# Chunked attention and a SwiGLU layer on one core: turning the second tile's tokens on VectorE and through DRAM instead of on TensorE

## The chip, the core and the metric

The kernel runs on 1 of the 8 cores of one Trainium2 chip. A core has TensorE (PE in the profile, its weight loads PEld), VectorE (DVE), ScalarE (ACT), GpSimd (POOL) and SyncE (SP), whose queue here issues nearly every DMA. The metric is the device time of one execution in microseconds (us), as the median of the runs shown.

## The reference

Attention runs within chunks of 64 tokens, for 8 batches, 8 heads and 576 tokens of head size 64. Its result, as 4608 tokens of 512 channels, goes through a normalised SwiGLU layer with 1536 hidden features, all in float32:

```python
scores = scale * np.matmul(q_c, k_c.transpose(0, 1, 2, 4, 3))
attn = np.exp(scores - np.max(scores, axis=-1, keepdims=True))
attn = attn / (np.sum(attn, axis=-1, keepdims=True) + 1e-09)
x = np.matmul(attn, v_c)            # then (B, H, S, D) -> (B * S, H * D)
...
rms = np.sqrt(np.mean(x * x, axis=-1, keepdims=True) + 1e-06)
xn = x / rms * rms_g
g = xn @ w_gate
silu = g * (1.0 / (1.0 + np.exp(-g)))
val = xn @ w_val
out = silu * val @ w_out
```

## The kernel before, in words

The 4608 tokens are 9 tiles of 512. Tiles 0, 1 and 2 are computed with plain products; the last six go in three pairs, by a scheme with seven products in place of eight, whose weight sums are prepared during tiles 1 and 2. Every float32 product is made of three products of a high and a low part (`xh`, `xl` for tokens, `parts` for weights).

A plain tile has 12 steps `f`. In each, TensorE makes the gate product `ps_g` (12 matmuls), the value product `ps_v` (12) and, one step late, the down product into the four banks `acc` (12, `down(f - 1)`). ScalarE applies the SiLU (`sg`), VectorE multiplies (`sg`), and the two split the result into `gh` and `gl`. The gate and value banks come from a pool of two, so `ps_g` of step f + 1 can start only when the SiLU of step f has read its bank. At the end of a tile, `evacuate` copies the four `acc` banks to `o`, on VectorE and ScalarE in turn, and SP stores them (`out_dram<-o`).

Tokens come in units of 256, two to a tile. Attention for the next tile runs in between the steps of the present one: scores (`ps_s<-kt,qt`), softmax, the values (`ps_o`), the normalisation, and then the tokens have to be turned, so that channels lie on partitions, before they are split into `xh` and `xl`. There are three ways to turn:

- Tile 0, units 0 and 1: TensorE transposes (`x_turn_unit`).
- Tile 1, units 2 and 3, made during tile 0: `norm_unit` writes them into the tile `x`; at the end of tile 0, `x_transpose` turns them with 16 TensorE transposes of 128x128, eight before `down(10)` and eight before `down(11)`, and ScalarE and VectorE split from PSUM.
- Units 4 and on: VectorE transposes 32x32 blocks in place in a tile `xu` (`turn_x`), one DMA stores it to DRAM (`away_x`), and four DMAs read it back into `x` with the blocks in their places (`turn_x_back`). The splits then read SBUF.

Also in tile 0, the float64 weights are converted, piece by piece (`conv_step`), on ScalarE and VectorE. From the converted parts, `save_plain` and `sides` in tile 1 store what the pairs need to DRAM (`wsd`, `osd`; `wsd<-parts` of 512 KB and `osd<-parts` of 256 KB each for the plain parts).

The order of the work is set by a scheduler, apart from stretches in `manual_schedule`, which keep the written order on the engines named. From tile 1 on, TensorE is in such a stretch. SP's queue is filled by the scheduler throughout tiles 0 to 2: it may place a DMA well ahead of, or behind, its place in the code. What stands in a queue is issued strictly in that order, and an entry that waits holds back all behind it.

In tile 2 the scores of unit 6 stand right behind the gate and value products of the first step; its tokens' loads are `qt`, `kt`, `vt` in `load_unit(6)`, which stand in the code at the start of tile 2.

Of the kernel before, what the change touches and what calls it, by code (L numbers as in the profile page):

```python
# [13 lines left out]
AF = mybir.ActivationFunctionType  # L14
# [71 lines left out]
def tile_chunk_attn_swiglu(  # L86
# [47 lines left out]
    def bank(pool, name):  # L134
        return pool.tile([P, 512], F32, tag=pool_tag[id(pool)], name=name)
# [320 lines left out]
    def turn_x(u):  # L456
        src = state["xu", u].rearrange("p q a s d -> p (q a s) d")
        nc.vector.transpose(src, src)
        src = state["xu", u].rearrange("p q a s d -> p q (a s d)")
        away = state["away", u] = dram.tile([P, 2 * DM], F32, name=f"away_x{u}")  # L460
        nc.sync.dma_start(away, src.rearrange("p q c -> p (q c)"))

    def turn_x_back(u, x):
        away = state["away", u]
        back = away.rearrange("(t p) (q r) -> q p t r", t=4, q=4)
        half = blocks(x)[:, 4 * (u % 2) : 4 * (u % 2) + 4]
        for q in range(4):
            nc.sync.dma_start(
                half[q * Q : (q + 1) * Q].rearrange("p t a c -> p t (a c)"), back[q]
            )  # L470

    def blocks(x):

        return x.rearrange("p s c -> p (s c)").rearrange("p (n a c) -> p n a c", a=NDT, c=2 * Q)
# [19 lines left out]
        nc.scalar.activation(spent, xs, AF.Square, accum_out=ss)  # L494
        return root(ss, "ri")

    def norm_unit(u, banks):
        rs = state.pop(("rs", u))
        subs = [state.pop(2 * u + s) for s in range(2)]
        first = 2 * u % NSUB  # L500
        xu = x[:, first : first + 2]
        xv = xu.rearrange("p s (j b a d) -> p j s b a d", j=2, b=2, d=Q)
        for j in range(2):
            for b in range(2):
                nc.vector.tensor_tensor(
                    xv[:, j, :, b],
                    banks[j].rearrange("p s (a b d) -> p b s a d", b=2, d=Q)[:, b],
                    rs[:, :, :, j].broadcast_to([P, 2, NPAIR, Q]),
                    op=ALU.mult,
                )  # L510
        ss = small.tile([P, 2], F32, name="ss_u")
        for s, st in enumerate(subs):
            spent = st["e"].rearrange("p a j k -> p (a j k)")
            nc.scalar.activation(spent, xu[:, s], AF.Square, accum_out=ss[:, s : s + 1])
        ri = root(ss, "ri_u")
        for s in range(2):
            nc.gpsimd.tensor_scalar(xu[:, s], xu[:, s], ri[:, s : s + 1], None, op0=ALU.mult)

    def x_split(dt, pt, cols):
        g = g_col[:, dt : dt + 1]  # L520
        hi, lo = xh[dt][:, cols], xl[dt][:, cols]
        if len(pt.shape) == 3:
            hi, lo = (w.rearrange("p (n c) -> p n c", c=2 * Q) for w in (hi, lo))
        nc.scalar.mul(hi, pt, g)
        nc.vector.scalar_tensor_tensor(
            lo, pt, g, hi.bitcast(F32), op0=ALU.mult, op1=ALU.subtract
        )

    def x_transpose(dts):
        for dt in dts:  # L530
            pt = bank(ps_a, "ps_x")
            for s in range(NSUB):
                nc.tensor.transpose(
                    pt[:, s * P : (s + 1) * P], x[:, s, dt * P : (dt + 1) * P], ident
                )
            x_split(dt, pt, slice(0, TT))

    def x_turn_unit(u, d, pool):
        pt = state["xt", u, d] = bank(pool, "ps_x")
# [96 lines left out]
    def gate_and_value(f):  # L636
        return up(wgh, wgl, f, "ps_g"), up(wvh, wvl, f, "ps_v")

    def gated(f, at, then, ps=None):
        pg, pv = ps or gate_and_value(f)  # L640
        if 0 in at:
            then()
        sg = tmp_tile("sg")
        gh = gp.tile([P, TT], F32R, name="gh")
        gl = gp.tile([P, TT], F32R, name="gl")
        with urgent():
            nc.scalar.activation(sg, pg, AF.Silu)
        if 1 in at:
            then()
        with urgent():  # L650
            nc.vector.tensor_tensor(sg, pv, sg, op=ALU.mult)
            nc.scalar.copy(gh, sg)
        if 2 in at:
            then()
        with urgent():
            nc.vector.tensor_tensor(gl, sg, gh.bitcast(F32), op=ALU.subtract)
        return gh, gl
# [561 lines left out]
        conv_sign(3)  # L1219
    conv_at[0] = EARLY  # L1220

    for t in range(PLAIN):
        if t == 1:
            ordered = tc.manual_schedule(engines={mybir.EngineType.PE})
            ordered.__enter__()
            at = {}
            for n, u in enumerate((4, 5)):
                for k, f in enumerate(unit_steps(u, x)):
                    at.setdefault(2 + 9 * n + FIRST_STEPS[k], []).append(f)
            half = Steps(at)  # L1230
            st = last.open("st", 1)
            made = [[] for _ in range(NF + 2)]
            for i in range(NPR):
                steps = sides(i, st)
                made[max(2 * i - 1, 0)].append(steps[0])
                made[2 * i].append(steps[1])
                made[2 * i + 1].append(steps[2])
        elif t == 2:
            st = last.open("st2", 1)
            x2 = st.tile([P, NSUB, DM], F32, tag="x2", bufs=1, name="x2")  # L1240
            at = {}
            for n, u in enumerate(range(2 * PLAIN, 2 * PLAIN + 4)):
                for k, f in enumerate(unit_steps(u, (x, x2)[n // 2])):
                    after_it = {1: LATE_STEPS, 2: LONG_STEPS}.get(n, UNIT_STEPS)
                    at.setdefault(max(UNIT_AT[n] + after_it[k], 0), []).append(f)
            for i in range(OUT_FIRST):
                for k, todo in enumerate(out_sides(i, st)):
                    at.setdefault(4 * i + 2 + k, []).extend(todo)
            one, two, late = x_sides(x, x2, st)
            for n, f in enumerate(one):  # L1250
                at.setdefault(15 + n, []).append(f)
            at.setdefault(22, []).extend([two[0], two[4]])
            at.setdefault(23, []).extend(two[1:4])
            early = {n: list(todo) for n, todo in enumerate(late)}
            for n, i in enumerate(range(OUT_FIRST, NPR)):
                for k, todo in enumerate(out_sides(i, st)):
                    early.setdefault(6 + 5 * n + k, []).extend(todo)
            at.setdefault(14, []).append(lambda: ring_load_ahead(0))
            half = Steps(at)
        acc = [ps_acc.tile([P, DM], F32, tag="acc", name=f"acc{s}") for s in range(NSUB)]  # L1260
        prev = None
        for f in range(NF):
            if f in gs:
                conv_step()
                g = gs.pop(f)
            else:
                g = gated(f, CONVS[f % 2], conv_step, ps.pop(f, None))
            if t == 0:
                if f in (0, 5):
                    u = 2 + (f == 5)  # L1270
                    load_unit(u)
                    sc = two_banks(ps_a, "ps_s")
                    for i in (2 * u, 2 * u + 1):
                        scores(i, sc)
                    if f:
                        softmax_rows(u, sc)
                    else:
                        softmax_whole(u, sc)
                elif f in (2, 7):
                    for i in (2 * u, 2 * u + 1):  # L1280
                        att_transpose(i)
                elif f in (3, 8):
                    o = two_banks(ps_a, "ps_o")
                    for i in (2 * u, 2 * u + 1):
                        att_values(i, o)
                    norm_unit(u, o)
                if f == NF - 1:
                    x_transpose((0, 1))
            elif t == 1 and f == NF - 1:
                for dt in range(NDT):  # L1290
                    x_split(dt, blocks(x)[:, :, dt], slice(0, TT))
            if t == 1:
                if f % 2 == 0:
                    save_plain(f // 2)
                for todo in made.pop(0):
                    todo()
            if t:
                half()
            if prev is not None:
                down(acc, f - 1, *prev)  # L1300
            if t:
                half()
            prev = g
        if t == 0:
            x_transpose((2, 3))
        down(acc, NF - 1, *prev)
        for s in range(NSUB):
            evacuate(acc, t, s)
# [84 lines left out]
```

## Time and profile before

| | |
|---|---|
| median of 3 runs | 899.57 us (899.17 to 899.58) |
| the profiled execution's own time | 898.29 us |
| its span in the trace | 896.5 us |
| TensorE busy | 880.0 us (98%) |
| VectorE busy | 607.6 us (68%) |
| ScalarE busy | 454.1 us (51%) |
| GpSimd busy | 185.7 us (21%) |

The span is what the trace covers from the first instruction to the last; the execution's own time has 1.8 us more around it. Busy shares are means over the span. A matmul's end in the trace is modelled, so matmuls that follow each other overlap a little, and it is the distance between two starts that tells what one costs.

### The profile page before, as it was taken

To read this page: it belongs to the slowest core of one execution; us is meant where nothing else is said; L and a number is where in the kernel's file an instruction comes from. 1 tells how busy PE (TensorE), PEld (TensorE's weight loads), DVE (VectorE), ACT (ScalarE), POOL (GpSimd) and SP (SyncE) were. 2 spreads that over 40 slices of the span, in tenths; PEclk is the share of its full clock that TensorE was granted. 3 is DMA by queue.
4 is the path that set the end of the run, shared out by engine and by line. 5 is a ranking of instruction groups with operands and counts; after the bars stand their busy time and mean duration, and the time that the engine had idled before them with its cause. 6 is when DMAs were issued, how large, how long until landed. Compare 5 with 4: busy or idle time off the path is not lost.

```text
span 896.5 us, 17443 instructions
## 1 busy us (share of the span) xinstructions
PE 880.0 (98%) x6828; PEld 720.6 (80%) x6828; DVE 607.6 (68%) x965; ACT 454.1 (51%) x772; POOL 185.7 (21%) x157
## 2 busy tenths in 40 slices
PE   5999999999999999999999999999999999999998
PEld 4778888888888888888887888888878888888886
DVE  6999955364568745985677997556769953334776
ACT  5988934253446464454456645435547522222452
POOL 0004050342200000233233003333330014323200
PEclk8899999999999999999999999999999999999999
DMA  9889999777978855698977877677667794445442
GB/s 349 328 318 336 332 337 347 239 255 235 303 252 234 267 170 196 250 298 294 320 240 265 318 301 286 245 277 249 232 231 286 281 355 171 152 154 199 179 165 95
DMA packets 85794, 231.84 MB, mean 259 GB/s; under 512 B 8912, under 2 KB 45264, under 8 KB 71504
## 3 DMA queue, kind: packets, MB, share of 16 engines
q1 hardware_dynamic: 84656, 230.20, 73.1%
q8 instruction: 54, 0.88, 0.4%
q10 hardware_dynamic: 1056, 0.52, 0.2%
q14 instruction: 28, 0.23, 0.1%
HBM read 167.25 MB, written 63.44 MB: 257 GB/s over the span
## 4 chain that ended last, share of the span: by engine, by line
PE 94%; DVE 2%; ACT 2%; DMA 0%; issue 0%; POOL 0%; ACTq 0%; DVEq 0%
PE ps_b L857 11%; PE ps_a L857 11%; PE ps_c L857 11%; PE acc L664 11%; PE ps_g L627 11%; PE ps_v L627 10%; PE ps_b L1070 6%; PE ps_c L1070 6%; PE ps_d L857 5%; PE ps_a L1070 5%; PE ps_d L1070 3%; PE ps_o L426 2%; PE ps_s L299 2%; PE ps_o L484 1%; DMA x<-qT_dram 0%; ACT raw L196 0%
## 5 line engine op out<-in xcount | busy, mean ns | idle before, releaser
L857 PE MATMUL ps_b<-xp,wr 128*128 128x512 f32 x432 | 104.7, 391 | 0.1
L857 PE MATMUL ps_c<-xp,wr 128*128 128x512 f32 x432 | 104.0, 390 | 0.0
L857 PE MATMUL ps_a<-xp,wr 128*128 128x512 f32 x432 | 103.8, 390 | 0.0
L627 PE MATMUL ps_g<-xh,parts 128*128 128x512 f32 x288 | 97.2, 399 | 0.1
L857 PEld LDWEIGHTS ps_b<-xp,wr 128*128 128x128 f32 x432 | 80.5, 188 | 17.4 <-issue 0.5
L857 PEld LDWEIGHTS ps_c<-xp,wr 128*128 128x128 f32 x432 | 80.9, 188 | 16.9
L627 PE MATMUL ps_v<-xh,parts 128*128 128x512 f32 x288 | 94.5, 389 | 0.0
L857 PEld LDWEIGHTS ps_a<-xp,wr 128*128 128x128 f32 x432 | 80.8, 188 | 17.0
L664 PE MATMUL acc<-parts,gh 128*128 128x512 f32 x288 | 90.2, 394 | 0.0
L945 POOL TENSOR_TENSOR g<-u,u 128x512 f32<-128x512 f32 x18 | 23.2, 1289 | 251.9 <-DVE u L941 141.3
L627 PEld LDWEIGHTS ps_g<-xh,parts 128*128 128x128 f32 x288 | 54.7, 190 | 12.7 <-ACT parts L237 0.6
L627 PEld LDWEIGHTS ps_v<-xh,parts 128*128 128x128 f32 x288 | 54.1, 188 | 11.2
L977 ACT CAST gh<-g 128x512 fp32r<-128x512 f32 x72 | 43.6, 622 | 37.8 <-PE ps_c L1070 13.5
L664 PEld LDWEIGHTS acc<-parts,gh 128*128 128x128 f32 x288 | 53.1, 188 | 11.3
L982 DVE TENSOR_TENSOR gl<-g,gh 128x512 fp32r<-128x512 f32 x72 | 49.3, 692 | 16.2 <-PE ps_a L1070 5.7
L913 ACT ACTIVATE p<-p 128x512 f32<-128x512 f32 x36 | 22.7, 632 | 70.0 <-POOL p L935 60.4
L935 POOL TENSOR_TENSOR p<-p,p 128x512 f32<-128x512 f32 x36 | 46.9, 1313 | 53.9 <-DVE rs L387 35.6
L627 PE MATMUL ps_g<-xl,parts 128*128 128x512 f32 x144 | 56.8, 395 | 0.1
L664 PE MATMUL acc<-parts,gl 128*128 128x512 f32 x144 | 56.1, 390 | 0.0
L627 PE MATMUL ps_v<-xl,parts 128*128 128x512 f32 x144 | 56.0, 389 | 0.0
L922 DVE TENSOR_TENSOR u<-ps_b,p 128x512 f32<-128x512 f32 x36 | 24.6, 687 | 41.5 <-PE ps_b L857 38.0
L857 PE MATMUL ps_d<-xp,wr 128*128 128x512 f32 x216 | 52.3, 391 | 0.0
(151 smaller groups left out, 1706.7 us busy)
## 6 DMA issues: line engine op xcount, KB each, us to landing
wr<-wsd SPq DMA_DIRECT2D x63, 1024.0 KB, 7.0
wo<-osd SPq DMA_DIRECT2D x30, 1024.0 KB, 7.6
raw<-w_up_dram SPq DMA_DIRECT2D x12, 1024.0 KB, 9.5
vt<-v_dram SPq DMA_DIRECT2D x18, 512.0 KB, 7.2
wsd<-parts SPq DMA_DIRECT2D x18, 512.0 KB, 8.3
qt<-qT_dram SPq DMA_DIRECT2D x17, 512.0 KB, 5.6
kt<-kT_dram SPq DMA_DIRECT2D x17, 512.0 KB, 6.6
away_e<-e SPq DMA_DIRECT2D x28, 256.0 KB, 3.5
```

The lines of the kernel that those rows point to most:

```text
L299: nc.tensor.matmul(st["s"][j][c * CH : (c + 1) * CH, pr], st["q"][rows, pr, tok : tok + CH], st["k"][rows, pr, tok : tok + CH], start=True ...
L426: nc.tensor.matmul(st["o"][(2 * c + t) * Q : (2 * c + t + 1) * Q, h * D : (h + 1) * D], eT[c][rows, t, h], vt[rows, c, h], start=True, sto ...
L627: nc.tensor.matmul(ps, a[f][:, cols], b[dt], start=(dt == 0 and i == 0), stop=(dt == NDT - 1 and i == 2),)
L664: nc.tensor.matmul(acc[s], a[:, cols], b, start=(f == 0 and i == 0), stop=(f == NF - 1 and i == 2),)
L857: nc.tensor.matmul(ps, w[:, a, m, cols], xp[:, b, kt], start=start and kt == 0 and i == 0, stop=stop and kt == 1 and i == 2, skip_group_ch ...
L913: nc.scalar.activation(t, t if src is None else src, AF.Silu)
L922: nc.vector.tensor_tensor(kp["u2"], b["b"], kp["p1"], op=add)
L935: nc.gpsimd.tensor_tensor(kp["p5"], kp["p1"], kp["p5"], op=add)
L945: nc.gpsimd.tensor_tensor(g[:, 0, 1], kp["u2"], kept[0]["u2"], op=mult)
L977: nc.scalar.copy(gh, src)
L982: nc.vector.tensor_tensor(gl, src, pair[0].bitcast(F32), op=ALU.subtract)
L1070: nc.tensor.matmul(banks[m][name], w[:, (0, 1, 0)[k], m * P : (m + 1) * P], (gh, gh, gl)[k], start=opens and i == 0 and k == 0, stop=not ( ...
```

## The change

Units 2 and 3 are now turned as the later units are, but in place: `norm_unit` writes the unit into the half of `x` in the block order that the later units use, VectorE transposes it there, SP stores that half to DRAM and reads it back into the same half in four reads. Unit 2 is turned at step 7 of tile 0 and read back at step 8; unit 3 is turned and read back at step 10. `x_transpose` is gone. The scaling of unit 3 by its norm goes from GpSimd to ScalarE (`shared`); that of unit 2 stays on GpSimd. At the last step of tile 0 the gate and the splits of the next tile keep their written order on ScalarE and VectorE. The rest of the diff puts output rows in order on the host.

```diff
-    def norm_unit(u, banks):
+    def norm_unit(u, banks, shared):
...
-        first = 2 * u % NSUB
-        xu = x[:, first : first + 2]
-        xv = xu.rearrange("p s (j b a d) -> p j s b a d", j=2, b=2, d=Q)
+        xu = x[:, 2 * u % NSUB : 2 * u % NSUB + 2].rearrange("p s c -> p (s c)")
+        xu = state["xu", u] = xu.rearrange("p (q a s d) -> p q a s d", q=4, a=NDT, s=2)
+        xv = xu.rearrange("p q (j b) s d -> p j s b q d", b=2)
+        xs = xu.rearrange("p q a s d -> p s (q a) d")
...
-            spent = st["e"].rearrange("p a j k -> p (a j k)")
-            nc.scalar.activation(spent, xu[:, s], AF.Square, accum_out=ss[:, s : s + 1])
+            spent = st["e"].rearrange("p a j k -> p (a j) k").rearrange("p a (b d) -> p (a b) d", d=Q)
+            nc.scalar.activation(spent, xs[:, s], AF.Square, accum_out=ss[:, s : s + 1])
         ri = root(ss, "ri_u")
         for s in range(2):
-            nc.gpsimd.tensor_scalar(xu[:, s], xu[:, s], ri[:, s : s + 1], None, op0=ALU.mult)
+            if shared:
+                nc.scalar.mul(xs[:, s], xs[:, s], ri[:, s : s + 1])
+            else:
+                nc.gpsimd.tensor_scalar(xs[:, s], xs[:, s], ri[:, s : s + 1], None, op0=ALU.mult)
...
-    def x_transpose(dts):
-        for dt in dts:
-            pt = bank(ps_a, "ps_x")
-            for s in range(NSUB):
-                nc.tensor.transpose(
-                    pt[:, s * P : (s + 1) * P], x[:, s, dt * P : (dt + 1) * P], ident
-                )
-            x_split(dt, pt, slice(0, TT))
...
+    def next_tokens():
+        for dt in range(NDT):
+            x_split(dt, blocks(x)[:, :, dt], slice(0, TT))
...
+            elif t == 0 and f == NF - 1:
+                ps_last = gate_and_value(f)
+                with tc.manual_schedule(engines={mybir.EngineType.Activation, mybir.EngineType.DVE}):
+                    g = gated(f, CONVS[f % 2], conv_step, ps_last)
+                    next_tokens()
...
-                    norm_unit(u, o)
-                if f == NF - 1:
-                    x_transpose((0, 1))
+                    norm_unit(u, o, u == 3)
+                if f in (7, 10):
+                    turn_x(2 + (f == 10))
+                if f in (8, 10):
+                    turn_x_back(2 + (f == 10), x)
             elif t == 1 and f == NF - 1:
-                for dt in range(NDT):
-                    x_split(dt, blocks(x)[:, :, dt], slice(0, TT))
+                next_tokens()
...
-        if t == 0:
-            x_transpose((2, 3))
```

Where the instructions stand, before and now, at three places.

**TensorE at the end of tile 0**, from the last matmuls of the last value product to `down(11)`; before:

```order
L627 MATMUL ps_v<-xl_126,parts 128x512
L627 MATMUL ps_v<-xh_122,parts 128x512
L533 MATMUL ps_x<-ident,x 128x128 x8
L664 MATMUL acc_566<-parts,gh 128x512 x2
L664 MATMUL acc_566<-parts,gl 128x512
L664 MATMUL acc_567<-parts,gh 128x512 x2
L664 MATMUL acc_567<-parts,gl 128x512
L664 MATMUL acc_568<-parts,gh 128x512 x2
L664 MATMUL acc_568<-parts,gl 128x512
L664 MATMUL acc_569<-parts,gh 128x512 x2
L664 MATMUL acc_569<-parts,gl 128x512
L533 MATMUL ps_x<-ident,x 128x128 x8
```

and now:

```order
L622 MATMUL ps_v<-xl_126,parts 128x512
L622 MATMUL ps_v<-xh_122,parts 128x512
L659 MATMUL acc_566<-parts,gh 128x512 x2
L659 MATMUL acc_566<-parts,gl 128x512
L659 MATMUL acc_567<-parts,gh 128x512 x2
L659 MATMUL acc_567<-parts,gl 128x512
```

Both groups of eight transposes are gone; nothing else of TensorE's order has changed, here or elsewhere.

**ScalarE in tile 0 at step 9**: the norm of unit 3 (`ss_u`), then the SiLU of step 9 (`sg`); before:

```order
L514 ACTIVATE e_1009,ss_u_1257<-x_127 128x512
L514 ACTIVATE e_1018,ss_u_1257<-x_127 128x512
L150 ACTIVATE ss_u_1257<-ss_u_1257 128x2
L647 ACTIVATE sg_1313<-ps_g_1277 128x512
L237 CAST parts_1310<-w_1208 128x1024
```

and now:

```order
L515 ACTIVATE e_1009,ss_u_1260<-x_127 128x512
L515 ACTIVATE e_1018,ss_u_1260<-x_127 128x512
L150 ACTIVATE ss_u_1260<-ss_u_1260 128x2
L519 ACTIVATE x_127<-x_127,ri_u_1263 128x16x32 x2
L642 ACTIVATE sg_1320<-ps_g_1284 128x512
L237 CAST parts_1317<-w_1211 128x1024
```

The two scalings of unit 3 have come in ahead of the SiLU, and they need the root that GpSimd takes in between.

**SP's queue from the end of tile 1 to the start of tile 2.** `away_x5` and the reads from it turn unit 5, the second half of tile 2's tokens; `qt_2623` and its `kt`, `vt` are unit 6's before, `qt_2620` and its `kt`, `vt` are unit 6's now. Before, ahead of the stores of the sums of weights (`side`, `w`):

```order
L754 DMA w_2327<-wfd11_139 128x1024
L267 DMA qt_2623<-qT_dram 128x1024
L461 DMA away_x5_2423<-xu_2395 128x1024
L268 DMA kt_2624<-kT_dram 128x1024
L269 DMA vt_2625<-v_dram 128x1024
L468 DMA x_127<-away_x5_2423 32x4x256 x4
```

and now:

```order
L749 DMA w_2322<-wfd10_138 128x1024
L749 DMA w_2324<-wfd11_139 128x1024
L461 DMA away_x5_2420<-xu_2392 128x1024
L682 DMA wsd17_157<-parts_1218 128x4x256
L682 DMA wsd19_159<-parts_1218 128x4x256
L682 DMA wsd20_160<-parts_1317 128x4x256
L737 DMA osd1_162<-parts_1329 128x2x256
L737 DMA osd4_165<-parts_1329 128x2x256
L737 DMA osd10_171<-parts_1329 128x2x256
L468 DMA x_127<-away_x5_2420 32x4x256 x4
```

Six stores of plain parts, which stood at the start of tile 1 before, have come in ahead of the reads of unit 5, with one more weight load ahead of `away_x5`, and unit 6's three loads have left this place. Eight stores of weight sums follow in both, and then the stores of tile 1's output. From there on, before:

```order
L967 DMA out_dram<-o_2569 128x512
L967 DMA out_dram<-o_2572 128x512
L967 DMA out_dram<-o_2575 128x512
L967 DMA out_dram<-o_2578 128x512
L267 DMA qt_2739<-qT_dram 128x1024
L849 DMA wr_3545<-wsd0_140 128x2048
L268 DMA kt_2740<-kT_dram 128x1024
L269 DMA vt_2741<-v_dram 128x1024
```

and now:

```order
L962 DMA out_dram<-o_2566 128x512
L962 DMA out_dram<-o_2569 128x512
L962 DMA out_dram<-o_2572 128x512
L962 DMA out_dram<-o_2575 128x512
L267 DMA qt_2620<-qT_dram 128x1024
L268 DMA kt_2621<-kT_dram 128x1024
L269 DMA vt_2622<-v_dram 128x1024
L267 DMA qt_2736<-qT_dram 128x1024
L844 DMA wr_3542<-wsd0_140 128x2048
```

Unit 6's `qt`, `kt` and `vt` now stand behind the last store of tile 1's output, where unit 7's `qt` stood before.

## Rows read from the trace of the kernel before

**Rows 1.** The view of busy time by stretches, 56 to 650 us, core 0.
```profile
core 0: us, PE busy (x) PEld busy (x) DVE busy (x) ACT busy (x) POOL busy (x), PEclk, DMA share, GB/s
...
56.00:650.00 594.00, 594.00 (x5176) 486.68 (x5175) 409.97 (x664) 310.55 (x544) 136.55 (x111) 1.00 0.80 272
```

**Rows 2.** Timeline of TensorE, last value product of tile 0 to tile 1.
```profile
128.30 0.39 PE L627 MATMUL ps_v<-xh,parts 128*128 128x512 f32 x1
...
138.24 0.39 PE L627 MATMUL ps_g<-xh,parts 128*128 128x512 f32 x1
```

**Rows 3.** The chain that ended last: start us, us, what.
```profile
117.58 2.72 PE ps_g L627 x12
```

**Rows 4.** Timeline of tile 0, three engines: start us, us, engine, line.
```profile
113.12 0.58 ACT L647 ACTIVATE sg<-ps_g 128x512 f32<-128x512 f32 x1
...
113.30 1.15 POOL L151 TENSOR_TENSOR ri_u<-ss_u,mhalf 128x2 f32<-128x2 f32 x1 [28.04 <-ACT ss_u L150]
...
131.29 0.69 DVE L651 TENSOR_TENSOR sg<-ps_v,sg 128x512 f32<-128x512 f32 x1 [6.09 <-PE ps_x L533]
```

**Rows 5.** Two single lines: ns min/median/max, first and last start us.
```profile
L458 DVE STREAM_TRANSPOSE xu<-xu x14: 1233/1246/1249, 184.9 to 666.7; 128x1024 f32<-128x1024 f32 x14
...
L452 ACT ACTIVATE xu<-xu,ri x28: 705/723/730, 183.1 to 665.9; 128x512 f32<-128x512 f32 x28
```

**Rows 6.** DMA issues, 140 to 250 us: KB each, median us to landing.
```profile
away_x<-xu SPq DMA_DIRECT2D x2, 512.0 KB, 4.6
...
x<-away_x SPq DMA_DIRECT2D x8, 128.0 KB, 4.3
...
wsd<-parts SPq DMA_DIRECT2D x2, 512.0 KB, 6.8
...
osd<-parts SPq DMA_DIRECT2D x3, 256.0 KB, 5.7
```

**Rows 7.** The timeline of SP's queue, from tile 1 to tile 2.
```profile
224.78 0.45 SPq L267 DMA_DIRECT2D qt<-qT_dram  x1
...
241.89 3.39 SPq L967 DMA_DIRECT2D out_dram<-o  x4
...
245.33 0.44 SPq L267 DMA_DIRECT2D qt<-qT_dram  x1
...
248.86 0.33 SPq L268 DMA_DIRECT2D kt<-kT_dram  x1
...
249.25 1.18 SPq L269 DMA_DIRECT2D vt<-v_dram  x1
```

**Rows 8.** DMA issues again: the last three loads of rows 7, one each.
```profile
qt<-qT_dram SPq DMA_DIRECT2D x1, 512.0 KB, 3.7
...
kt<-kT_dram SPq DMA_DIRECT2D x1, 512.0 KB, 6.0
...
vt<-v_dram SPq DMA_DIRECT2D x1, 512.0 KB, 6.8
```

**Rows 9.** The timeline of three engines where tile 2 begins.
```profile
243.45 0.59 ACT L964 COPY o<-acc 128x512 f32<-128x512 f32 x1 [0.67 <-DMA wsd<-side]
...
243.76 0.68 DVE L966 COPY o<-acc 128x512 f32<-128x512 f32 x1
...
247.62 1.16 PE L299 MATMUL ps_s<-kt,qt 64*64 64x64 f32 x64
```

**Rows 10.** Busy time by stretches: tile 1's end, and an early one.
```profile
224.00:242.00 18.00, 18.00 (x81) 14.92 (x80) 7.94 (x12) 8.63 (x18) 6.63 (x6) 1.00 1.00 318
...
16.00:20.00 4.00, 2.09 (x23) 1.53 (x26) 3.79 (x10) 3.36 (x6) 0.12 (x1) 0.68 1.00 418
```

**Rows 11.** The timeline of TensorE in its first 33 us.
```profile
16.91 0.66 PE L357 MATMUL ps_t<-ident,e 128*128 128x128 f32 x4 [2.02 <-ACT e L316]
...
27.41 0.80 PE L627 MATMUL ps_g<-xh,parts 128*128 128x512 f32 x1
...
32.23 0.40 PE L627 MATMUL ps_v<-xh,parts 128*128 128x512 f32 x1
```

More of the change, by code (lines that the diff above doesn't have):

```diff
@@ L1390 @@
     rows = np.concatenate([rows[: PLAIN * TT], pairs])
-    turned = rows[2 * TT :].reshape(-1, 4, 2, Q, DM).transpose(0, 2, 1, 3, 4).reshape(-1, DM)
-    return np.concatenate([rows[: 2 * TT], turned])
+    turned = rows[TT:].reshape(-1, 4, 2, Q, DM).transpose(0, 2, 1, 3, 4).reshape(-1, DM)
+    return np.concatenate([rows[:TT], turned])
```

## The prediction

> **What bounds the kernel now.** I first read the busy time by stretches. From 56 to 650 us TensorE is busy for all 594.00 us at a granted clock of 1.00, its upper level of 2.4 GHz, and the DMA engines have a share of .80 [rows 1]. The change lies inside this stretch. So the work of VectorE, ScalarE and SP counts only where TensorE comes to wait for it, and a wait there is not made good later, since no idle time stands behind it to take it up. What has to be found is (1) which TensorE work goes away and (2) where TensorE now arrives ahead of its data. For (1) I read TensorE's timeline at the end of tile 0, for (2) the rows of ScalarE, VectorE and SP at the three places that the order of the instructions shows.
>
> **What is removed.** From the first `ps_v` matmul of tile 0's last step, at 128.30, to the first `ps_g` matmul of tile 1, at 138.24, are 9.94 us [rows 2]. In between stand `ps_v` (12 matmuls), `down(10)` (12), `down(11)` (12) and 16 transposes. Twelve matmuls of this size take 2.72 us [rows 3], so 36 take 8.16, and the transposes are left with 9.94 - 8.16 = 1.78 us. With TensorE never idle there, all of it is gained: **-1.8 us**.
>
> **What is added to the engines.** VectorE gets two transposes of 1.25 us, ScalarE two scalings of 0.72 us each for unit 3 [rows 5], which GpSimd loses. VectorE stood idle for 6.09 us at the end of tile 0, waiting for `ps_x` [rows 4]; this covers its 2.5 us. Without such a cover they would cost at most their own 2.5 + 1.4 us.
>
> ScalarE's two scalings matter by their place, ahead of the SiLU of step 9, which now also waits behind them for the root on GpSimd. The root starts at 113.30 and takes 1.15 [rows 4]: 114.45. Two scalings end at 115.9, the SiLU of 0.58 us [rows 4] at 116.5. It has to have read its bank when `ps_g` of step 10 starts at 117.58 [rows 3]. Queued behind the SiLU are VectorE's product and the splits for `down(9)`, which comes a step later. About 1.1 us of slack is left, so I cost this at nothing; another 1.1 us of lateness would use it up.
>
> Unit 3's way: its scalings end at 115.9, VectorE's transpose ends near 117.4, the store to DRAM takes 4.6 and the reads back 4.3 us [rows 6], with some issue time in between some 127 to 128. Its splits are wanted just ahead of tile 1's first `ps_g`, now 138.24 - 1.78 = 136.5. Some 8 us of cover: nothing. Unit 2 is read back two steps sooner and has more. That the splits no longer wait for `ps_x` in PSUM can't gain, because TensorE did not wait for them.
>
> **What is moved.** The cost that I see is in SP's queue. Unit 6's `qt` is issued at 224.78 before [rows 7], with `kt` and `vt` behind it, some 20 us ahead of the scores of unit 6 at 247.62 [rows 9]. Now the three stand behind the last store of tile 1's output, in the seat in which unit 7's loads stood. The stores can't be issued sooner than `o` is copied from PSUM. The four take SP from 241.89 for 3.39 us, and `qt` of unit 7 follows at 245.33 [rows 7]. It lands 3.7 us later [rows 8]: 249.03. In that seat `kt` landed at 248.86 + 6.0 = 254.86 and `vt` at 249.25 + 6.8 = 256.05 [rows 7, 8], so loads in a row land about 1.2 us apart; unit 6's `kt`, now right behind its `qt`, is due at 249.03 + 1.2 = 250.2. (All in the times of before; TensorE, the copies and the stores move by the same -1.78, so that the distance stays.) The scores want it at 247.62: **a wait of 2.6 us** at `ps_s<-kt,qt`. TensorE works in order, so all products behind it wait too.
>
> The lower bound of this wait: the loads are issued at the very end of the last copy of `o`, 243.76 + 0.68 = 244.44 [rows 9], 0.9 us sooner than 245.33. Then it is 1.7.
>
> The upper bound: more DMA work stands ahead. Six plain stores (3 of 512 KB, 3 of 256 KB) [rows 6] and a weight load of 128x1024 floats, 512 KB, have come in, while unit 6's three loads of 512 KB are gone from ahead [rows 8]: 1536 + 768 + 512 - 1536 = 1280 KB, 1.31 MB. The DMA engines are full (share 1.00) from 224 to 242 and move 318 GB/s [rows 10]. So the surplus takes 4.1 us, and passed on one for one the wait is 2.6 + 4.1 = 6.7 us. That lateness in this queue reaches the seat at all is seen before: the last copy of `o` on ScalarE is held for 0.67 us by a store of sums of weights [rows 9].
>
> In the page "DMA: Bandwidth & Descriptors", section "Queues, rings and completion order", the Trainium skill says that each DMA engine takes the descriptors of one issuing queue in the order of its ring; by this rule all stores ahead have to go first, the 4.1 us pass in full, and the sum would be -1.8 + 6.7 instead of the one below. Both the copy's 0.67 us wait and the full share speak for it; no row of before shows a surplus passed whole.
>
> I choose **4.2 us**, halfway between 1.7 and 6.7. The full share and the 0.67 us wait draw it up. What draws it down is that the stores of `o` and unit 6's loads are tied to the copies, not to the queue's length: the part of the surplus that drains before the copies, or beside the wait for them, costs nothing.
>
> The same stores delay the reads of unit 5, which the first `ps_g` of tile 2 needs. A wait there, a tile's step ahead of the scores, does not add to the other: TensorE passes the scores when `kt` is there, however it spent the time before.
>
> **The sum** is -1.8 + 4.2 = +2.4 us. The profiled execution's own time of 898.29 us becomes 900.7. The median of the runs shown, 899.57, lies 1.28 above that execution, which gives 902.0 us. With the bounds of the wait the main case reaches from 899.5 (1.7) to 904.5 (6.7).
>
> **The rivals.**
>
> *The clock falls after the wait.* Early in the kernel, `ps_t` comes after 2.02 us of waiting for ScalarE [rows 11], and the granted clock means .68 over 16 to 20 us, between the levels of 1.2 and 2.4 GHz [rows 10]. Twelve `ps_g` matmuls then took from 27.41 to 32.23, that is 4.82 us [rows 11], against 2.72 [rows 3]: 2.1 us more for one such stretch. For it speaks that a wait of 4 us is longer than that one; against it that TensorE has been busy without a gap for a long time ahead of it here, and that it was still warming up there. One stretch at the lower level gives 902.0 + 2.1 = 904.1. The Trainium skill's page "TensorE: Matmul & The Clock Gate", section "HAM oscillation — how this bites in real kernels", tells of a kernel whose TensorE waits for a DMA between bursts and starts each next burst at the low clock; whether one wait of this size does so, no run here shows yet.
>
> *The whole surplus passes.* The stores ahead go strictly first and the wait is 6.7: 904.5. For it speaks the full share at 224 to 242, against it that this stretch also holds loads which nobody waits for.
>
> *Only just late.* The wait is its lower bound, 1.7 us, and pays back just what the transposes gave: 899.5.
>
> *The other side: the moved loads cost nothing.* If `kt` lands by the time at which the scores now stand, 247.62 - 1.78 = 245.84, only the saving is left: 897.8. With 3.7 + 1.2 us to land, its `qt` would have to be issued by about 240.9 in the new times, ahead of the first store of `o`, at 241.89 before and near 240.1 now. It needs the four stores to go out in under 1 us instead of 3.39, or a much quicker landing than 3.7. Those stores follow copies, and these follow the last matmuls, which I don't see change.
>
> *A wait elsewhere.* The SiLU behind the scalings is late, or unit 3 reads back late behind other stores of tile 0, or the plain stores that have gone into tile 1 hold up unit 5's scores. A price of 1.5 us, about the length of the two scalings, on top of the sum: 903.5.
>
> **How the numbers follow.** A change of 0.2%, 1.8 us, is about what a measurement of this kernel can tell from none: 897.8 to 901.4 counts as the same. The main case (902.0) has .33, of which .09 lies below 901.4; the clock (904.1) .22; the whole surplus (904.5) .12; only just late (899.5) .12, all of it the same; nothing (897.8) .10, .09 of it faster; a wait elsewhere (903.5) .11, of which .04 lies within the same where the wait for `kt` is short. That makes .09 faster, .01 + .09 + .12 + .04 = .26 the same, and .24 + .22 + .12 + .07 = .65 slower. The range from 898.4 to 905.0 leaves out the pure saving below, and above it a large wait together with a fallen clock, some 2 in 10 together.
>
> **What would show it right or wrong.** Right: no `ps_x` matmul at the end of tile 0, and 8.16 us from the last step's first `ps_v` matmul to tile 1's first `ps_g`; SP issuing unit 6's `qt` right behind the fourth store of `o`; a row `ps_s<-kt,qt` at tile 2's start with 3 to 6 us of idle time ahead of it, ended by the DMA `kt`; SiLU of step 9 read before `ps_g` of step 10. The granted clock in the 10 us behind that wait decides the clock rival: 1.00 throughout, or .5. I am wrong if TensorE has no idle time at those scores, or if its idle time is at other rows: `ps_g` of step 10 in tile 0, tile 1's first `ps_g`, or unit 5's scores in tile 1. If the wait is there but outside 1.7 to 6.7 us, the share of the surplus was wrong, not the mechanism.

## The result and the profile after

The changed kernel takes 912.58 us (median, 911.43 to 913.93) against 899.37 of the kernel before: a ratio of 1.0149 (95% interval 1.0131 to 1.0166). It is slower by 13.2 us; 902.0, with 898.4 to 905.0, was forecast. The profiled execution's own time is 913.93 us, its span 912.1.

The page's first part and two of its DMA lines; for each engine busy us, share and instructions, for the queue packets, MB and share:

```profile
PE 883.9 (97%) x6812; PEld 722.2 (79%) x6812; DVE 614.9 (67%) x967; ACT 456.0 (50%) x774; POOL 180.9 (20%) x155
...
q8 instruction: 54, 0.88, 0.4%
...
q14 instruction: 28, 0.23, 0.1%
```

What TensorE waited for, in total, times and the longest, in us (waits of the first 20 us left out):

```profile
PE ps_o L426 <- issue: 5.9, 2, 4.2
PE ps_s L299 <- DMA kt<-kT_dram: 4.5, 1, 4.5
...
PE ps_g L622 <- DVE xl L529: 0.6, 2, 0.3
```

TensorE's timeline at the places that count, to be read beside [rows 2, 9]:

```profile
128.81 0.39 PE L622 MATMUL ps_v<-xh,parts 128*128 128x512 f32 x1
...
136.97 0.39 PE L622 MATMUL ps_g<-xh,parts 128*128 128x512 f32 x1
...
242.05 0.49 PE L622 MATMUL ps_g<-xh,parts 128*128 128x512 f32 x1 [0.27 <-ACT xh L528]
...
246.07 0.39 PE L622 MATMUL ps_v<-xh,parts 128*128 128x512 f32 x1
...
253.48 1.99 PE L299 MATMUL ps_s<-kt,qt 64*64 64x64 f32 x64 [4.50 <-DMA kt<-kT_dram]
...
421.84 1.47 PE L426 MATMUL ps_o<-vt,eT 64*32 64x64 f32 x127
...
427.47 0.26 PE L426 MATMUL ps_o<-vt,eT 64*32 64x64 f32 x1 [4.16 <-issue]
...
673.35 1.40 PE L426 MATMUL ps_o<-vt,eT 64*32 64x64 f32 x119
...
676.48 0.32 PE L426 MATMUL ps_o<-vt,eT 64*32 64x64 f32 x9 [1.73 <-issue]
```

Where the time went is read best from the starts of the same instruction in both traces, since idle time and slow matmuls both show in them:

| from the start of | before | after | later by | new at this step |
|---|---|---|---|---|
| last step's `ps_v`, tile 0 | 128.30 | 128.81 | +0.51 | |
| first `ps_g` of tile 1 | 138.24 | 136.97 | -1.27 | -1.78 |
| first `ps_g` of tile 2 | 242.08 | 242.05 | -0.03 | +1.24 |
| `ps_v` behind it | 244.80 | 246.07 | +1.27 | +1.30 |
| `ps_s` of unit 6 | 247.62 | 253.48 | +5.86 | +4.59 |
| `ps_g` behind it | 248.71 | 255.40 | +6.69 | +0.83 |
| `ps_v` behind that | 251.56 | 259.95 | +8.39 | +1.70 |
| `ps_a` behind the halted `ps_o` | 415.18 | 427.66 | +12.48 | +3.97 |
| `ps_c` behind that | 418.04 | 432.94 | +14.90 | +2.42 |
| `ps_d` behind the second halt | 660.30 | 676.73 | +16.43 | +1.97 |

The rest, -0.3 us, is spread between these. Four blocks, then: the transposes, -1.8; the lateness of unit 5's reads and unit 6's loads, 1.24 + 1.30 + 4.59 = 7.1; the slow matmuls behind that wait, 2.5; and two halts inside `ps_o` groups of the pairs, with slow matmuls behind the first, 8.4. The waits of the three `ps_g` matmuls sum to only 0.9 us, of the 2.5 that the starts show.

TensorE in stretches: busy, count, granted clock, DMA share, GB/s. The clock is at the lower level behind the wait for `kt` and behind the first halt, not behind the second:

```profile
core 0: us, PE busy (x), PEclk, DMA share, GB/s
...
253.40:256.00 2.60, 2.52 (x66) 0.50 1.04 436
256.00:260.00 4.00, 4.00 (x13) 0.62 0.90 327
260.00:264.00 4.00, 4.00 (x19) 1.00 0.18 26
421.80:428.00 6.20, 2.04 (x130) 0.86 0.98 384
428.00:431.00 3.00, 3.00 (x8) 0.50 0.92 388
...
677.00:681.00 4.00, 4.00 (x19) 1.00 0.13 49
```

SP's queue where [rows 7] stood:

```profile
228.86 2.72 SPq L682 DMA_DIRECT2D wsd<-parts  x3
231.62 3.90 SPq L737 DMA_DIRECT2D osd<-parts  x3
235.62 2.45 SPq L468 DMA_DIRECT2D x<-away_x  x4
...
243.20 0.85 SPq L775 DMA_DIRECT2D wsd<-w  x1
244.14 2.98 SPq L962 DMA_DIRECT2D out_dram<-o  x4
247.21 0.56 SPq L267 DMA_DIRECT2D qt<-qT_dram  x1
247.82 0.44 SPq L268 DMA_DIRECT2D kt<-kT_dram  x1
```

And unit 3 in tile 0, on ScalarE, VectorE and TensorE:

```profile
114.89 1.34 ACT L519 ACTIVATE x<-x,ri_u 128x512 f32<-128x512 f32 x2 [1.28 <-POOL ri_u L151]
116.13 0.58 ACT L642 ACTIVATE sg<-ps_g 128x512 f32<-128x512 f32 x1
...
116.26 1.25 DVE L458 STREAM_TRANSPOSE x<-x 128x1024 f32<-128x1024 f32 x1 [0.25 <-ACT x L519]
...
117.93 0.39 PE L622 MATMUL ps_g<-xh,parts 128*128 128x512 f32 x1
```

### The profile page after: what moved, and what is told of

The parts are those of the page before. It is cut to its first block, busy times and chain, and to the rows that moved or that the text cites. A ratio compares the mean times of both kernels' runs of the same rounds, so it can differ in the third digit from the quotient of the medians.

```text
span 912.1 us, 17437 instructions
## 1 busy us (share of the span) xinstructions
PE 883.9 (97%) x6812; PEld 722.2 (79%) x6812; DVE 614.9 (67%) x967; ACT 456.0 (50%) x774; POOL 180.9 (20%) x155
## 4 chain that ended last, share of the span: by engine, by line
PE 72%; issue 10%; DMA 7%; DVE 5%; POOL 3%; ACT 2%; SPq 2%; DVEq 0%; POOLq 0%; ACTq 0%
PE ps_a L852 11%; PE ps_b L852 11%; PE ps_c L852 11%; PE ps_d L852 5%; PE ps_c L1065 5%; PE ps_b L1065 5%; PE ps_a L1065 5%; PE acc L659 4%; PE ps_g L622 4%; PE ps_v L622 3%; PE ps_d L1065 3%; PE ps_o L426 2%; PE ps_s L299 2%; DMA x<-away_x 1%; DVE w L774 1%
## 5 line engine op out<-in xcount | busy, mean ns | idle before, releaser
L852 PE MATMUL ps_a<-xp,wr 128*128 128x512 f32 x432 | 106.3, 397 | 0.0
```

The lines of the kernel that those rows point to most:

```text
L852: nc.tensor.matmul(ps, w[:, a, m, cols], xp[:, b, kt], start=start and kt == 0 and i == 0, stop=stop and kt == 1 and i == 2, skip_group_ch ...
```

## The halts: a theory before the experiments

The halts are ended by nothing that the profile shows: "issue". Three things point to TensorE's own program. The page shows 54 packets of the queue for instructions, 0.88 MB, so 16 KB each; TensorE's 6812 matmuls and 6812 weight loads, shared out over 54, are 252 to a packet. (That this queue is TensorE's follows from the sizes: 0.88 MB over the 13816 records that the trace has of TensorE, its sequencer's 192 among them, is about 64 bytes each, and so is the 0.23 MB of `q14` over the 3621 records of all other engines.) A `ps_o` group of a unit is 128 matmuls with 128 weight loads, about one packet's worth, and passes in 1.5 us. And the first halt comes behind matmul 127 of 128. In that stretch the DMA engines were full (share .98 above) with `qt`, `kt`, `vt` and two loads `wr` of 1 MB, issued from 420.24 on. The packet shows in the DMA view of 424.8 to 425.8, inside the halt:

```profile
q8 instruction: 1, 0.02, 6.0%
```

In the kernel before, the packet for this place shows in 409.5 to 410.5, ahead of the group, which starts at 413.33 and passes without a halt:

```profile
q8 instruction: 1, 0.02, 7.4%
```

```profile
413.33 1.92 PE L426 MATMUL ps_o<-vt,eT 64*32 64x64 f32 x128
```

The Trainium skill's page "Runtime: NRT & Kernel Launch", section "Instruction fetch mechanics", has the same size, blocks of 16 KiB or 256 instructions, and calls the cost of crossing from one to the next mostly hidden. Here it isn't where a group uses up a block in 1.5 us.

Theory A, then: the change took 32 instructions out of TensorE's program at the end of tile 0 (6828 - 6812 = 16 transposes, and 16 weight loads), so that from there on every block ends at another instruction, and one of these ends now falls at the end of a `ps_o` group. Theory B: the halts follow from the lateness or the added DMA traffic.

## The experiments

Ratios are to the kernel before, run on the same chip.

**1. The kernel before without the transposes.**

```diff
-            pt = bank(ps_a, "ps_x")
-            for s in range(NSUB):
-                nc.tensor.transpose(
-                    pt[:, s * P : (s + 1) * P], x[:, s, dt * P : (dt + 1) * P], ident
-                )
-            x_split(dt, pt, slice(0, TT))
+            x_split(dt, x[:, dt], slice(0, TT))
```

> The kernel before without the 16 transposes of units 2 and 3; the splits read the unturned tokens from SBUF, so the turning of tile 1's tokens is left out. Nothing goes through DRAM for it, and unit 6's loads stay ahead of the stores of the weight sums. Theory A (place of TensorE's instruction loads): TensorE's program is 32 instructions shorter from the end of tile 0 on, 16 transposes and their 16 weight loads, as in the changed kernel, so the halts inside the ps_o groups (4.16 us near 427 and 1.73 near 676 in the changed kernel, ended by nothing that the profile shows) come here too, with no wait for kt ahead of them: 899.4 - 1.8 + 6 to 8.5 = 903.5 to 906. Theory B (the halts follow from the lateness that the wait for kt brings, or from the added DMA traffic): no halt, only the transposes are gained: 897.6.

906.38 us, ratio 1.0070 (1.0049 to 1.0091). No DMA was added and `kt` is not waited for, yet the halts are there, the first again behind matmul 127. Theory B falls for them. Of ten executions one took 898.53, 8 us less than the median; its trace was not taken. TensorE's timeline:

```profile
412.93 1.47 PE L426 MATMUL ps_o<-vt,eT 64*32 64x64 f32 x127
419.35 0.31 PE L426 MATMUL ps_o<-vt,eT 64*32 64x64 f32 x1 [4.96 <-issue]
```

**2. The changed kernel, unit 6's loads early.** With `EARLIER = 600`:

```diff
+        with tc.high_priority(offset=EARLIER) if u == 6 else nullcontext():
-        nc.sync.dma_start(qt, qT[u])
-        nc.sync.dma_start(kt, kT[u])
-        nc.sync.dma_start(vt, v[u])
+            nc.sync.dma_start(qt, qT[u])
+            nc.sync.dma_start(kt, kT[u])
+            nc.sync.dma_start(vt, v[u])
```

> The changed kernel with unit 6's three loads issued earlier, among the stores of weight sums ahead of unit 5's away_x; every other order unchanged. Both theories: the 4.50 us wait for kt at tile 2's first scores goes, and with it the low clock behind it (0.83 us in ps_s and 1.70 us in ps_g): 7.1 us less. The waits of tile 2's first ps_g for the splits (2.5 us by the starts) stay or grow by up to 4 us, since 1.5 MB more stand ahead of unit 5's reads. Theory A: the halts inside ps_o stay: 905 to 909. Theory B: they go too: 896.5 to 900.

912.05 us, ratio 1.0148 (1.0126 to 1.0170): outside what either theory gave. The wait for `kt` went and another took its place: the work that stands behind the loads came later. ScalarE's split `side` waited 3.88 us for a plain store, as the trace has it, VectorE's sums `w` waited for `side`, and behind them in VectorE's order stood the product `sg` of tile 1's last step, which the split `gh` needs. ScalarE, VectorE, then TensorE:

```profile
237.71 1.14 ACT L774 CAST side<-w 128x512 fp32r<-128x512 f32 x2 [3.88 <-DMA wsd<-parts]
...
238.36 2.90 DVE L776 TENSOR_TENSOR w<-w,side 128x512 fp32r<-128x512 f32 x2 [6.61 <-ACT side L774]
...
242.56 1.22 PE L661 MATMUL acc<-parts,gh 128*128 128x512 f32 x2 [3.94 <-ACT gh L649]
```

By the starts, tile 2's first `ps_g` moved by 6.5 us at this place. From 226 us of the kernel before to 257 the changed kernel lost 9.5 us and this one 6.6, so the edit gave back about 3, and most of the loss stayed. So it is not the seat of the loads alone that costs, but also the DMA work in the stretch. The halts stayed (4.95 and 0.60 us). The medians, 912.58 and 912.05, show little of the 3 us; the changed kernel's profile is its slowest execution.

**3. The changed kernel with 16 small matmuls at the end of tile 0.**

```diff
+    def spare(count):
+        pt = bank(ps_a, "spare")
+        for _ in range(count):
+            nc.tensor.matmul(pt[:D, :CH], ident[:D, :D], ident[:D, :CH], start=True, stop=True)
...
+                spare(16)
```

> The changed kernel with 16 small matmuls of 64x64 at the end of tile 0, whose result nobody reads: 32 instructions of TensorE, as many as the transposes took, for about 0.3 us by the 1.16 us of 64 such matmuls at ps_s. Unit 6's loads stand as late as in the changed kernel. Theory A: the place of TensorE's instruction loads is that of before, so the halts inside ps_o go, and the wait for kt stays: 912.6 - 8.4 + 0.3 = 904.5. Theory B: all stays: 912 to 913.

908.30 us, ratio 1.0111 (1.0096 to 1.0126). The halts are gone, the wait for `kt` is there with 4.68 us: as theory A has it. The size was off by my own count: TensorE runs each of these matmuls as two, so that 64 instructions came in, 32 more than before, and they took 2.07 us where I had 0.3.

```profile
133.17 2.07 PE L1220 MATMUL spare<-ident 64*64 64x64 f32 x32
```

**4. Both edits.**

> Both edits, the early loads of unit 6 and the 16 small matmuls. Theory A: no wait for kt and no halt in ps_o: 912.6 - 7.1 - 8.4 + 0.3 = 897.4, up to 901 if tile 2's first ps_g waits longer. Theory B: as with the early loads alone, plus 0.3.

903.68 us, ratio 1.0061 (1.0042 to 1.0081). This is above the 901 that theory A allowed. No halt, no wait for `kt`, but again `acc` waits for `gh`, 2.8 us, and tile 2's first `ps_g` comes 4.9 us later by the starts. The medians give the early loads 4.6 us against experiment 3, where they gave 0.5 in experiment 2; by the starts over the same stretch they give about 3 in both (8.1 us lost in experiment 3, 5.0 here). The granted clock fell behind this wait too, to the lower level:

```profile
244.57 0.73 PE L661 MATMUL acc<-parts,gh 128*128 128x512 f32 x2 [2.82 <-ACT gh L649]
```

```profile
core 0: us, PE busy (x), PEclk, DMA share, GB/s
246.00:249.00 3.00, 3.00 (x9) 0.50 1.07 394
```

**5. The kernel before with unit 6's loads in the late seat, and nothing else moved.**

```diff
+        if u == 6:
+            for first in (qt[:, 0, :1], kt[:, 0, :1], vt[:, 0, 0, :1]):
+                nc.vector.tensor_copy(first, state["o"][:, :1])
...
+        if t == 1:
+            state["o"] = o
```

> The kernel before with unit 6's three loads held until VectorE's last copy of o in tile 1 is done (three one-column copies from that o into qt, kt and vt), so that they stand behind the stores of o as in the changed kernel; no other store has moved, and TensorE's program is that of before. Theory Q (the seat costs 1.7 to 2.6 us, and the lateness above that in the changed kernel is the surplus of stores ahead, passed on): a wait for kt of 1.7 to 2.6 us, none at the splits, 899.0 + 2.6 and up to 2.5 us of low clock behind it: 901 to 904. Theory R (the seat alone makes the whole lateness, 7.1 us by the starts in the changed kernel): 906 to 908.6. No halt in ps_o by either.

902.90 us, ratio 1.0049 (1.0034 to 1.0065). This prices the seat: a wait of 2.79 us, where the prediction worked out 2.6; the granted clock was 1.00 from 250.80 to 254.00 in this profile. The profiled execution, 900.63 us, is the fastest of the four; the others took 901.91 to 904.45, and what they lost besides is not known.

```profile
250.84 1.16 PE L302 MATMUL ps_s<-kt,qt 64*64 64x64 f32 x64 [2.79 <-DMA kt<-kT_dram]
```

**6. The first experiment with 8 small matmuls.** They are of 64x32 by 64, in the four column groups in turn, so that they overlap.

```diff
+    def spare():
+        pt = bank(ps_a, "spare")
+        for n in range(8):
+            out = slice(n % 4 * Q, (n % 4 + 1) * Q)
+            cols = slice(n // 4 * D, (n // 4 + 1) * D)
+            nc.tensor.matmul(pt[out, cols], ident[:CH, :Q], ident[:CH, :D], start=True, stop=True)
```

> The kernel before without the transposes, as the first experiment (the turning of tile 1's tokens left out), with 8 matmuls of 64x32 by 64 at the end of tile 0 that nobody reads; by the trace such a matmul is two in TensorE's program, each with a weight load, so the 8 are 32 instructions, as many as the 16 transposes were, for 0.2 us. Theory A (place of the instruction loads): the halts in ps_o are gone: 899.0 - 1.8 + 0.2 = 897.4. If the halts had another cause, 906.4 as without the small matmuls.

897.97 us, ratio 0.9988 (0.9979 to 0.9997); ten executions lie between 896.49 and 898.80. Beside the first experiment only these matmuls have come in (and some stores and softmax steps of tile 1 changed places): 8.4 us and both halts are gone, at 6828 matmuls as before. (The two ran on different chips, on which the kernel before took 899.04 and 899.01.) Of the transposes' 1.8 us only 0.3 is left here at their place, by the starts, since `acc` waits 0.48 us there for `gl` and the small matmuls take some. This is the pair that shows theory A.

```profile
132.16 0.43 PE L1222 MATMUL spare<-ident 64*32 64x64 f32 x16
...
414.08 1.48 PE L426 MATMUL ps_o<-vt,eT 64*32 64x64 f32 x128
```

The order of TensorE's records agrees to the instruction. In the changed kernel the two halts come at records 7361 and 11713, which are 4352 = 17 x 256 apart; in experiments 1, 2 and 7 they come at the same two numbers, to within one. The record 256 places ahead of the first, with which by theory A that block begins, stands at 421.62, right where the `ps_o` group begins: TensorE is through the whole block in 1.5 us, and the packet for the next one starts 3.5 us behind the block's start. In the kernel before, the record of the same number stands 34 places sooner in the program (16 transposes, 16 weight loads, two of the sequencer), among the long matmuls, at 409.62; the packet shows within 1 us of it, 3 us ahead of the group.

**7. The changed kernel with its last six plain stores in tile 2.**

```diff
-                if f % 2 == 0:
+                if f % 2 == 0 and f < NF - 2:
                     save_plain(f // 2)
...
+            if t == 2 and f == 2:
+                save_plain(NPR - 1)
```

> The changed kernel with the last six plain stores (those ahead of unit 5's reads) written in tile 2 instead of at the end of tile 1; unit 6's qt and kt then stand ahead of unit 5's reads again. Theory: no wait for kt and none at tile 2's first splits, so the 2.5 and 7.1 us are gone; the halts in ps_o stay, 6 to 8.4 us: 903 to 906.

906.99 us, ratio 1.0096 (1.0078 to 1.0113). Unit 6's `qt` and `kt` went back ahead of unit 5's reads, the waits at tile 2's start went (1.5 us by the starts is left), and the halts stayed, 2.73 us right behind the first `ps_o` group and 2.01 inside the second. A new wait came, `ps_o` near 383 for `eT`, 1.5 us.

**8. The same with the 8 small matmuls.**

> The same with the 8 small matmuls, so that TensorE's program has the length of before from the end of tile 0 on. Theory: no wait and no halt, only the transposes' 1.8 us less 0.2 are left: 897.4, faster than before by 0.1 to 0.3%. If the added DMA traffic costs something elsewhere, or if the moved stores collide with tile 2's loads: 899 or more.

901.11 us, ratio 1.0026 (1.0016 to 1.0035). No halt; against experiment 7, on the same chip, the small matmuls give 5.9 us. What is left is the wait for `eT`, 1.6 us and by the starts 3.7, with the granted clock at .50 from 386.1 to 389.4. The moved stores have also changed where 1 MB loads `wr` stand among the turns of unit 10; that this makes the wait is read from the order.

**9. Those turns given priority.** In `turn` and `turn_back`, for units 9 and 10:

```diff
+        with tc.high_priority(offset=EARLIER) if i // 2 in (9, 10) else nullcontext():
```

> The kernel of the eighth experiment with the DMAs that turn the attention weights of units 9 and 10 (away_e and the reads eT) given priority in the order, so that no 1 MB load wr stands between them. Theory: the 1.6 us wait of ps_o for eT near 383 and the low clock behind it go, 3.7 us by the starts: 901.1 - 3.7 = 897.4, faster than before by 0.1 to 0.3%. Rival: the new order, which also moves splits of VectorE and ScalarE in tile 2, makes another wait there: 899 to 903.

906.47 us, ratio 1.0093 (1.0078 to 1.0108): the rival, and beyond its range. Splits on ScalarE and VectorE came later in the new order, and TensorE came to wait in several new places of the first pair: 1.0 us for `p`, 1.0 and 0.9 us for `xp`, and still 1.4 us for `eT`.

**10. The late seat with few stores ahead.** Experiment 8 with the edit of experiment 5.

> The changed kernel with the 8 small matmuls, with the last plain stores put into tile 2 (two of 512 KB still stand ahead of unit 5's reads, where the changed kernel has 2.25 MB in six) and with unit 6's loads held until VectorE's last copy of o. Theory Q (the lateness above the seat's own is the surplus of stores): the wait for kt is that of the seat alone, 2.8 us as in the fifth experiment, and none at the splits: 899.0 - 1.8 + 0.2 + 2.8 = 900.2, up to 902.7 with a low clock. If the late loads cost 7 us with few stores ahead too: 904 to 907.

903.30 us, ratio 1.0054 (1.0037 to 1.0070). The wait for `kt` is 3.81 us. Wait and time lie between the two cases that were expected: more than the seat alone with a fallen clock, up to 902.7, and less than the whole lateness, from 904.

```profile
252.20 1.07 PE L302 MATMUL ps_s<-kt,qt 64*64 64x64 f32 x41 [3.81 <-DMA kt<-kT_dram]
```

With the waits of `ps_g` ahead, by the starts, the lateness at these scores is 2.85 us with none of the plain stores ahead (experiment 5), 4.43 with two of them, 1.05 MB (this one), and 7.13 with six, 2.36 MB (the changed kernel). That is 1.5 us a MB for the first two and 2.1 for the other four, a half to two thirds of the 3.1 us that 318 GB/s [rows 10] make. One more weight load of 512 KB stands ahead in the last two.

**11. Experiment 8 with the six stores at step 10 of tile 2.**

```diff
-            if t == 2 and f == 2:
+            if t == 2 and f == 10:
```

> The kernel of the eighth experiment with its six plain stores written at step 10 of tile 2 instead of step 2, so that the loads and turns of units 6 to 10 keep the order that they have before. Theory: neither the wait of ps_o near 383 nor one for kt, and no halt; only the transposes' 1.8 us less 0.2 are left: 898.7 - 1.6 = 897.1, faster than before by 0.1 to 0.3%. Rival: the stores now delay the turning of unit 9, which stands behind them: 898.5 to 902.

898.58 us against 898.84, ratio 0.9993 (0.9983 to 1.0002): no difference from the kernel before. Neither a halt nor a wait for `kt` or `eT` is left. By the starts of this execution 1.0 us is lost at tile 2's first `ps_g`, and 1.2 us at the first `ps_v` of the kernel, near 32 us; the second also shows in profiles of experiments 3, 4, 9 and 10. In these five the granted clock is at .50 from 31.0 to 33.5, where it is .97 in the kernel before; what keeps it down there, I have not tried.

## Why the prediction was wrong

Of the 13.8 us between the 16.2 of the four blocks and the +2.4 of the forecast, 8.4 are the halts, for which the sum had no term, 2.9 the lateness at tile 2's start, which it had too small, and 2.5 the clock, which it left to a rival.

**The saving was right.** From the last step's first `ps_v` to tile 1's first `ps_g` there are now 136.97 - 128.81 = 8.16 us, as worked out, and no wait is in between.

**The hidden work was hidden.** The SiLU of step 9 starts at 116.13 and ends at 116.7, 0.2 us later than forecast, and `ps_g` of step 10 starts at 117.93 without a wait. Tile 1's first `ps_g` did not wait for unit 3 either.

**The place of the cost was right, its size was not.** `kt` ends a wait at tile 2's scores, behind the fourth store of `o`. The step that failed here is "halfway between 1.7 and 6.7": the lateness is 7.1 us, above my upper bound (the wait for `kt` alone, 4.50, lies inside). With the times of before moved by -1.27, `qt` was due at 244.06 and came at 247.21, 3.15 later: SP reached the stores of `o` only at 244.14, since the queue ahead of them was late. Then `kt` landed 253.48 - 247.21 = 6.27 us behind the issue of `qt`, where I had 3.7 + 1.2 = 4.9. Together 2.6 + 3.15 + 1.37 = 7.1. Passing the whole surplus was a rival, with 6.7, and comes nearer; but that it comes so near is in part luck. The surplus was worked out with unit 6's three loads taken off. In experiment 5 these have left too and nothing has come in, and the lateness is no less than the seat's 2.6. Above that case 2.36 MB of stores and a weight load of 0.52 MB stand ahead in the changed kernel, 9.1 us at 318 GB/s, and 4.3 were lost: so part did drain, as I argued, but from a larger surplus. That the lateness grows with the stores ahead is shown by experiments 5 and 10, that moving the loads alone gives back only a part by experiment 2. The sentence that a wait at `ps_g` "does not add" holds: 2.5 us of the 7.1 were spent there.

**The clock came on top, not instead.** I gave it 2.1 us as a rival to the main case; behind the wait of 4.50 us it cost 0.83 + 1.70 = 2.5, with a granted clock of .50. It also fell behind the waits of 4.16 (the halt), 4.68 (experiment 3) and 3.81 us (experiment 10: 1.6 us by the starts). These four are what the Trainium skill's page "TensorE: Matmul & The Clock Gate", section "HAM oscillation — how this bites in real kernels", tells of, a burst that starts at the low clock behind a wait; the trace agrees. Behind shorter waits it went either way: it stayed at 1.00 behind 2.79 (experiment 5), 2.73 (experiment 7) and 1.73 us (the second halt), and fell to .50 behind 2.82 (experiment 4), behind second halts of 2.03 and 2.01 (experiments 1 and 7) and behind 1.6 us in two parts (experiment 8). So the length of a wait alone does not decide it in these runs.

**The halts were missed altogether.** This is the larger failed step. "With TensorE never idle there, all of it is gained" looked only at the stretch in which the transposes stood. Taking 32 instructions out moved the ends of all blocks of TensorE's program behind them, and 8.4 us were lost at 427 and 676, in a part of the kernel that the change does not touch. Experiments 1, 3 and 6 show it in both directions, and 7 and 8 once more. What I have from the trace alone, and did not try, is why the packet is late: that it waits among the loads `qt`, `kt`, `vt` and `wr`. One of the ten executions of experiment 1 took no longer than the kernel before, so the place of the block makes the halts likely, not certain.

The four blocks make -1.8 + 7.1 + 2.5 + 8.4 = 16.2, against 912.1 - 896.5 = 15.6 in the spans; the medians lie 13.2 apart, and the profiled execution is the slowest of the four.

## What to carry to other kernels

A stretch in which the DMA engines are full had no free seat here: moving the loads in it gave back 3 us of 8 to 10 and moved the rest of the wait to other work, while taking the added stores out of the stretch (experiments 7, 8 and 11) removed this wait. Taking instructions out of an engine's program moves everything behind them in the blocks by which it is loaded; after such a change look for waits that nothing explains in groups of many short instructions, and try again with a few instructions added. A gain of 1.8 us can be real at its place and still not be found in the total: with both repaired, the changed kernel equals the one before.

## What the runs showed of the hardware that was not expected

TensorE can halt for its own program: 0.6 to 5.0 us at the end of a group of 128 matmuls that passes in 1.5 us otherwise, where a block of 256 instructions begins at or shortly ahead of the group and the 16 KB packet for the next block shows only behind the group's start. The small float32 matmuls of experiments 3 and 6 count as two in the trace, each with a weight load (16 in the code are 32 rows); a float32 transpose of 128x128 counts as one.
